# Attention with two mixtures of experts: products by low parts at the end of their group, and another spread of the next expert's weight split over a block

## The chip, the cores and the metric

The kernel runs on one core of a Trainium2 chip. The metric is the device time of one execution in microseconds, the median of several runs: 742.46 us before the change (three runs, 737.96 to 743.23). The engines' names: PE is TensorE (PEld its weight loads), DVE VectorE, ACT ScalarE, POOL GpSimd, SP SyncE, which issues most DMAs. PEq, ACTq and so on are the engines' sequencers, which run branches and semaphores.

## What is computed

Three stages in fp32. Attention over 2 batches of 8 heads, 1152 keys of 64 values, with the queries averaged in pairs; then two mixtures of experts over the 1152 tokens of 512 values that come out, each with 8 experts and a hidden width of 1024:

```python
attn = softmax(scale * q_pool @ k.transpose(0, 1, 3, 2))        # q_pool: queries averaged in pairs
x = rows(attn @ v)                                              # 1152 x 512
expert_idx = np.argmax(x @ w_gate, axis=1)                      # MoE 1, at most 288 tokens of an expert
h = np.maximum(np.einsum('ecd,edf->ecf', disp, w1), 0.0)
y = np.einsum('ecf,efd->ecd', h, w2)
out[i] = gate_w[i] * y[expert_idx[i], pos[i]]
do_compute = skip_score > 0                                     # MoE 2, with its own router
for e in range(E):
    h = np.maximum(xc[mask] @ w1[e], 0.0)
    y[mask] = gate_w[mask, None] * (h @ w2[e])
out[do_compute] = xc + y
```

## The kernel before

Attention takes the first 340 us or so, the experts of MoE 1 about 344 to 518, the last block of MoE 1 with the second router 518 to 565, and the experts of MoE 2 565 to 725. Then the last rows are written.

**Numbers in two parts.** The experts' products are made in fp32r, which keeps fewer bits, so each fp32 operand is held as a high part (its first twelve bits) and a low part (the rest). A product of two operands is the sum of three: high by high, high by low, low by high. For the tokens the parts are `xx[:, 0]` and `xx[:, 1]`, for the hidden layer `hh` and `hl`, for the weights the tiles `hi` and `lo` of each half (half 0 is w1, half 1 is w2).

**An expert's block.** `block_t` does up to 128 tokens of one expert. `first(hf)` lists the 12 products (4 chunks of the contraction, 3 parts) for one half of the hidden layer, and the relu behind them on ACT (L942, tile `hs`). `turn(hf)` transposes that half on PE (L948, `pg`), copies its high part on ACT (L950, `hh`) and takes the low part by subtraction on DVE (L951, `hl`). `second(py, hf)` lists the 12 products of that half by w2. PE's order in a block: first(0), half of first(1), turn(0), the rest of first(1), half of second(0), turn(1), a transpose of the next expert's tokens (`xprep`, L913 to L918, tiles `psx` and `xxn`), the rest of second(0), four products of second(1), a second such transpose (`xx`, for a second chunk of this expert), the other eight. The result is scaled on DVE (`yt`, L991 in MoE 1, L993 in MoE 2), the rows' places are worked out on DVE (`ix`, L883) and POOL issues the indirect DMA that writes the rows (L886).

**What fills a block.** Meanwhile the next expert's weights (four raw pieces of 1 MB, read by SP at L143) are split in 16 steps of 128x512. Step u copies the high part on ACT (L818, `hi`) and, one step behind, step u-1's low part is subtracted: on POOL for steps 0, 3, 6, 8, 11 and 14, on DVE for the other ten (L808, `lo`). Four steps use up one raw piece. The low part that ends a piece in half 0 issues the load that takes over its buffer; those of half 1 are kept back until after the branch. The steps are a list `fill`, and `flush(fill, n)` writes the next n of them into the program at that point. Each engine works its instructions off in the order in which they are written, and waits for other engines by semaphores; so the calls of `flush` set the order on ACT, DVE and POOL. The low parts that a `flush` puts out are one step behind the high parts.

**Between blocks.** Behind each expert's block stands a branch (L1172, in `experts`): if the expert has more than 128 tokens a second chunk follows, in `block_t` or, for up to 64 tokens, `block_h`. In this data that is so for experts 3 and 6 of MoE 1 and 6 of MoE 2. In the other eleven blocks that carry a split, the code of the second chunk is jumped over. `hs` has one buffer, and relu of the next block waits on ACT until DVE has passed L1172.

Of the kernel before, what the change touches and what calls it, by code (L numbers as in the profile page):

```python
# [8 lines left out]
F32 = mybir.dt.float32  # L9
F32R = mybir.dt.float32r  # L10
BF16 = mybir.dt.bfloat16
# [5 lines left out]
P = 128  # L17
# [4 lines left out]
def fused_kernel(  # L22
# [21 lines left out]
    KD = DM // P  # contraction chunks of the first product  # L44
    KF = F // P  # and of the second
    KC = S // P  # key chunks
    QP = 96  # rows of a chunk of queries, as loaded
    QC = SQ // QP
    CH = [P] * (SQ // P) + ([SQ % P] if SQ % P else [])  # token chunks of a batch
    NCH = len(CH)  # L50
    NT = B * NCH
    ROW = DM + 8  # a dispatched row: the token, its gate, its index
    REG = N  # rows of an expert's region
    NPRE = 3  # chunks of an expert that are read without an index
# [8 lines left out]
    # ---------------------------------------------------------------- constants  # L63
# [6 lines left out]
    rev = consts.tile([P, NT, E], F32, name="rev")  # E - e  # L70
# [10 lines left out]
    tri = consts.tile([P, P], BF16, name="tri")  # tri[k, m] = 1 where k < m  # L81
# [9 lines left out]
    def load_small(zeros):  # L91
        """Steps: the routers' weights, the capacity, zeros where tokens may be missing."""
# [22 lines left out]
        def capacity_value():  # L115
            # low + 2^32 * (high + (low < 0)), and not below 0
# [12 lines left out]
    # ---------------------------------------------------------------- weights  # L129
    RW = KD * F // 2  # words of a partition in one load: half of w1[e] or of w2[e]  # L130
# [15 lines left out]
    # ---------------------------------------------------------------- routing  # L146
# [5 lines left out]
    def masks(m):  # L152
        """1 in the rows of an expert's chunks that have no token."""
        nc.vector.tensor_tensor(
            out=mask[m],
            in0=cnt[m].unsqueeze(2).to_broadcast([P, E, NPRE]),
            in1=rowid.unsqueeze(1).to_broadcast([P, E, NPRE]),
            op=ALU.is_le,
        )

    def route(sp, ps_r, lg, nt, gate_out, prev, do=None, half_rows=()):
        """Three steps: the expert of each token, one-hot; its place among that expert's tokens; its gate.

        lg [P, nt, >= E] in SBUF; prev: one-hots of earlier tokens. The dictionary that is returned gets
        the one-hots (oh), the place (rank) and the first row of the expert's region (base).
        """
# [74 lines left out]
    def together(*lists):  # L241
        """The steps of several lists in turn."""
        n = max(len(x) for x in lists)
        for i in range(n):
            for x in lists:
                if i < len(x):
                    x[i]()

    def logits(m, rows, lg, ta, tb, xt, lt, groups, on_scalar=lambda j: j and j % 2, j0=0):
        """Steps to the logits of chunks of 128 tokens: for each group of chunks (each in a quadrant of the  # L250
        partitions) the transposes, the product and the way back."""
# [36 lines left out]
    def in_line(groups):  # L288
        """The steps of logits() in a row, a group's last ones behind the first transpose of the next."""
# [6 lines left out]
    def add_rows(ps, rows, places, first, last):  # L296
        """Adds to ps the transpose of the rows, each in its place: exact, by products with 0 and 1."""
# [10 lines left out]
    def places_of(place, oh):  # L308
        """One-hots of the tokens' places among an expert's first 128."""
# [3 lines left out]
    def count(ps_r, ohs, limit, m):  # L313
        """Tokens of each expert, on every partition, and in row 0 as integers."""
# [11 lines left out]
    def warm(ps, n):  # L326
        """Products that nobody reads: the array's clock would fall while it waits."""
# [24 lines left out]
    # ================================================================ attention  # L352
# [10 lines left out]
    def gate(b, ta, tb, groups):  # L363
        """Routing of a batch's tokens, and their rows to their experts' regions: steps to the logits, and the rest."""
# [31 lines left out]
    with ExitStack() as actx:  # L396
# [16 lines left out]
        PARTS = [(0, 2), (2, NCH)]  # chunks of the two halves of a pair's product with v  # L413
# [24 lines left out]
        def split0(n):  # L438
            """Sums of the pairs of queries, as far as the loads allow ahead."""
# [5 lines left out]
        def split1(n):  # L445
            """High and low parts of a head's keys and scaled queries, in twelve bits each: a list of steps."""
# [34 lines left out]
        def prep(n):  # L481
            """[high; low] of a head's keys, and [high; high], [low; low] of its queries, on the partitions."""
# [32 lines left out]
        def scores(n, c, it):  # L515
            """Scores of a chunk of queries with all keys; their maximum, exponentials and sums.

            The third piece of every chunk has a bank of its own, the others alternate.
            """
# [4 lines left out]
            def mm(j, part):  # L524
                # in the shared chunk the second head's queries have zeros in front of them
# [60 lines left out]
        def turn(n, c):  # L586
            """A chunk's weights with the keys on the partitions, in three groups."""
# [28 lines left out]
        def mix(i, part):  # L616
            """A pair of heads' product with v, turned to tokens on the partitions and divided by the sums."""
# [50 lines left out]
        # -------------------------------------------------------- the order of issue  # L668
# [25 lines left out]
        # The order of issue beside each of a pair's items, in the first pair and in the others: scores (s), the  # L694
        # maximum (m), the exponentials of the first pieces (f) and the last item's others (e), transposes of an
# [642 lines left out]
```

## Time and profile before

| what | us |
|---|---|
| runs: median (lowest to highest) | 742.46 (737.96 to 743.23) |
| span of the profiled execution | 734.7 |
| PE busy | 666.5 (91%) |
| DVE, ACT, POOL busy | 450.1, 433.3, 257.3 |
| lows on DVE (155) and POOL (101) | 157.2 and 142.0 |
| highs on ACT (256) | 141.5 |

The times are of one profiled execution, counted from the span's start. A row of an operation gives its line, the engine, output and inputs by the program's names, and shapes. Idle time is that of the engine just before the operation, with what ended it behind an arrow. PE's operations overlap their neighbours, so their starts are the better clock: two products in a row start about 0.23 us apart though each is listed with 0.4 us. Consecutive equal operations can stand in one row with their count.

### The profile page before, as it was taken

To read this page: it belongs to the slowest core of one execution; us is meant where nothing else is said; L and a number is where in the kernel's file an instruction comes from. 1 tells how busy PE (TensorE), PEld (TensorE's weight loads), DVE (VectorE), ACT (ScalarE), POOL (GpSimd) and SP (SyncE) were. 2 spreads that over 40 slices of the span, in tenths; PEclk is the share of its full clock that TensorE was granted. 3 is DMA by queue.
4 is the path that set the end of the run, shared out by engine and by line. 5 is a ranking of instruction groups with operands and counts; after the bars stand their busy time and mean duration, and the time that the engine had idled before them with its cause. 6 is when DMAs were issued, how large, how long until landed. Compare 5 with 4: busy or idle time off the path is not lost. (4 is left out here: it accounts for less than half of the span.)

```text
span 734.7 us, 11243 instructions
## 1 busy us (share of the span) xinstructions
PE 666.5 (91%) x3978; PEld 485.9 (66%) x3978; DVE 450.1 (61%) x729; ACT 433.3 (59%) x961; POOL 257.3 (35%) x240
## 2 busy tenths in 40 slices
PE   7999999999999999988888998899769888888994
PEld 6766667666767666646666766676648666666673
DVE  5755656565656664564888548842175788888211
ACT  5876767676757676651777347722350677776210
POOL 4322222222222520053566226510165566665010
PEclk8999999999999999999999999999988999999998
DMA  6042624050202122033889618850454798884100
GB/s 179 31 138 104 212 104 167 17 196 17 81 17 82 67 71 78 16 123 114 302 314 331 246 35 311 278 201 19 147 186 147 259 318 303 315 302 162 32 30 13
DMA packets 55599, 111.39 MB, mean 152 GB/s; under 512 B 5470, under 2 KB 14686, under 8 KB 55488
## 3 DMA queue, kind: packets, MB, share of 16 engines
q1 hardware_dynamic: 52128, 102.27, 40.8%
q0 software_dynamic: 3360, 7.72, 2.8%
q8 instruction: 59, 0.97, 0.5%
q14 instruction: 52, 0.43, 0.2%
HBM read 93.51 MB, written 19.71 MB: 154 GB/s over the span
## 5 line engine op out<-in xcount | busy, mean ns | idle before, releaser
L808 POOL TENSOR_TENSOR lo<-raw,hi 128x512 fp32r<-128x512 f32 x101 | 142.0, 1409 | 115.6 <-ACT hi L818 113.2
L808 DVE TENSOR_TENSOR lo<-raw,hi 128x512 fp32r<-128x512 f32 x155 | 157.2, 1065 | 4.3 <-ACT hi L818 4.3
L818 ACT CAST hi<-raw 128x512 fp32r<-128x512 f32 x256 | 141.5, 626 | 0.6 <-PE py L958 0.6
L527 PE MATMUL s_ps<-kop,qop 128*128 128x384 f32 x480 | 125.5, 369 | 1.7 <-ACT a L571 1.4
L555 DVE TENSOR_REDUCE m<-s_ps 128x1 f32<-128x1152 f32 x72 | 97.7, 1357 | 24.6 <-PE s_ps L527 22.4
L601 PE MATMUL pt<-ident,a 128*128 128x128 f32 x648 | 109.8, 283 | 3.2 <-ACT kop L476 1.1
L571 ACT ACTIVATE a<-s_ps,m 128x384 f32<-128x384 f32 (+1 forms) x144 | 106.8, 747 | 3.1 <-DVE m L555 2.9
L476 ACT COPY at<-pt 128x384 f32<-128x384 f32 x144 | 68.2, 481 | 64.0 <-PE pt L601 63.9
L601 PEld LDWEIGHTS pt<-ident,a 128*128 128x128 f32 x648 | 71.5, 140 | 45.9 <-ACT at L476 13.0
L627 PE MATMUL pv<-at,vr 128*64 128x320 f32 (+1 forms) x576 | 97.9, 428 | 0.0
L938 PE MATMUL ph<-hi,xxn 128*128 128x512 f32 x224 | 77.1, 405 | 13.1 <-PEq L1172 10.4
L476 DVE COPY at<-pt 128x384 f32<-128x384 f32 x72 | 39.8, 553 | 76.2 <-PE pt L601 74.1
L951 DVE TENSOR_TENSOR hl<-pg,hh 128x512 fp32r<-128x512 f32 x42 | 28.9, 687 | 89.0 <-ACT hh L950 89.0
L958 PE MATMUL py<-hi,hl 128*128 128x512 f32 x168 | 67.8, 404 | 12.5 <-DVE hl L951 12.5
L942 ACT ACTIVATE hs<-ph 128x512 f32<-128x512 f32 x42 | 25.1, 598 | 91.0 <-PE ph L938 52.3
L527 PEld LDWEIGHTS s_ps<-kop,qop 128*128 128x128 f32 x480 | 75.1, 187 | 5.3 <-ACT a L571 3.8
L958 PE MATMUL py<-hi,hh 128*128 128x512 f32 x168 | 68.7, 409 | 0.6
L886 POOL DMA_INDIRECT out_dram<-yt,ix x23 | 22.6, 981 | 133.0 <-DVE ix L883 81.7
L958 PE MATMUL py<-lo,hh 128*128 128x512 f32 x168 | 67.7, 403 | 0.0
L466 POOL TENSOR_TENSOR qhl<-qr,qhl 96x384 fp32r<-96x384 f32 x30 | 29.9, 1016 | 95.7 <-DVE qhl L464 95.7
L938 PEld LDWEIGHTS ph<-hi,xxn 128*128 128x128 f32 x224 | 42.1, 188 | 27.3 <-ACTq L1172 12.1
L454 POOL TENSOR_TENSOR khl<-kr_None,khl 128x576 fp32r<-128x576 f32 x14 | 19.8, 1414 | 87.2 <-DVE khl L453 87.2
(170 smaller groups left out, 948.2 us busy)
## 6 DMA issues: line engine op xcount, KB each, us to landing
raw<-in_moe_w_dram SPq DMA_DIRECT2D x64, 1024.0 KB, 6.0
x<-xs SPq DMA_DIRECT2D x36, 260.0 KB, 6.3
xs<-xtok SPq DMA_DIRECT2D x8, 780.0 KB, 7.4
qr<-in_q_dram SPq DMA_DIRECT2D x16, 288.0 KB, 3.2
vr<-in_v_dram SPq DMA_DIRECT2D x8, 576.0 KB, 6.0
kr_None<-in_k_dram SPq DMA_DIRECT2D x7, 576.0 KB, 5.0
out_dram<-xtok SPq DMA_DIRECT2D x3, 768.0 KB, 7.7
x<-out_dram SPq DMA_DIRECT2D x4, 512.0 KB, 6.3
```

What stands on the lines that cost most here:

```text
L466: sub.tensor_tensor(out=t[:, 1, :, r, :], in0=qs, in1=t[:, 0, :, r, :].bitcast(F32), op=ALU.subtract)
L476: (nc.vector.tensor_copy if on_vector else nc.scalar.copy)(dst, src)
L527: i = nc.tensor.matmul(s_ps[0:M, bank[j], 0 : 3 * P], qop[n + r][:, part, o : o + M], kop[n + r][:, j, :], start=(part == 0 and r == (c == ...
L555: i = nc.vector.tensor_reduce(out=nm, in_=s_ps[:, lo : lo + 3, 0 : 3 * P], axis=AX.XY, op=ALU.max, negate=True)
L571: i = nc.scalar.activation(a[:, a0 : a0 + nb, :], s_ps[:, b0 : b0 + nb, 0 : 3 * P], AF.Exp, bias=nm, accum_out=t[:, c, n % 2, k : k + 1],)
L601: nc.tensor.transpose(ps[:, x * P : (x + 1) * P], a[:, g, x * P : (x + 1) * P], ident)
L627: nc.tensor.matmul(hold["pv"][j * D : (j + 1) * D, 0:w], vrt[i][:, j, c * D : (c + 1) * D], at_t[2 * i + j, part][:, c, :], start=(c == 0) ...
L808: eng.tensor_tensor(out=lo, in0=raw, in1=hi.bitcast(F32), op=ALU.subtract)
L818: nc.scalar.copy(hi, raw)
L938: lambda d=d, i=i, a=a, b=b: nc.tensor.matmul(ps, xx[:, a, d, :], w1[b][:, d, s], start=(d + i == 0), stop=(d == KD - 1 and i == 2))
L951: nc.vector.tensor_tensor(out=hl[:, fs, :], in0=ps, in1=hh[:, fs, :].bitcast(F32), op=ALU.subtract)
L958: lambda f=f, i=i, a=a, b=b: nc.tensor.matmul(py, a[:, f, :], w2[b][:, f, :], start=(f + i == 0), stop=(f == KF - 1 and i == 2))
```

## The change

In `first` and `second` the loop over the three parts becomes the outer one: four products high by high, four by the other operand's low part, and then four by the tokens' (or the hidden layer's) low part, where they went in threes before. In the flow of a block, four steps of `fill` come ahead of the first product, then two (as before), one, one, two, three and the rest, where it was two, three, two, two, three and the rest. The rest of the difference takes comments out. In the numbering after the change, lines from 964 on are one higher (L1172 is L1173).

```diff
             def first(hf):
                 mms = []
-                for d in range(KD):
-                    for i, (a, b) in enumerate(((0, 0), (0, 1), (1, 0))):
+                for i, (a, b) in enumerate(((0, 0), (0, 1), (1, 0))):
+                    for d in range(KD):
                         mms.append(
                             lambda d=d, i=i, a=a, b=b: nc.tensor.matmul(
                                 ps, xx[:, a, d, :], w1[b][:, d, s], start=(d + i == 0), stop=(d == KD - 1 and i == 2)
...
             def second(py, hf):
                 mms = []
-                for f in range(hf * 4, hf * 4 + 4):
-                    for i, (a, b) in enumerate(((hh, 0), (hh, 1), (hl, 0))):
+                for i, (a, b) in enumerate(((hh, 0), (hh, 1), (hl, 0))):
+                    for f in range(hf * 4, hf * 4 + 4):
...
+            flush(fill, 4)
             mms, relu = first(0)
             flush(mms, 12)
             relu()
             flush(fill, 2)
             mms, relu = first(1)
             flush(mms, 6)
             turn(0)
-            flush(fill, 3)
+            flush(fill, 1)
             flush(mms, 12)
             relu()
-            flush(fill, 2)
+            flush(fill, 1)
             py = pa([P, DM], "py")
             mms = second(py, 0)
             flush(mms, 6)
             turn(1)
             flush(preps, 1)
             flush(fill, 2)
             flush(mms, 12)
             mms = second(py, 1)
             flush(fill, 3)
             flush(mms, 4)
             flush(preps, 1)
             flush(fill, len(fill))
             flush(mms, 12)
```

ACT in the first expert's block of MoE 1, from the block's first relu to its last high part, before (`hi_1_0` is the high part of expert 1's w1, `hi_1_1` of its w2):

```order
L942 ACTIVATE hs<-ph 128x512
L818 CAST hi_1_0_3845<-raw_1_0_0_3562 128x512 x2
L950 CAST hh<-pg 128x512
L818 CAST hi_1_0_3845<-raw_1_0_0_3562 128x512 x2
L818 CAST hi_1_0_3845<-raw_1_0_1_3590 128x512
L942 ACTIVATE hs<-ph 128x512
L818 CAST hi_1_0_3845<-raw_1_0_1_3590 128x512 x2
L950 CAST hh<-pg 128x512
L917 CAST xxn<-psx 128x512
L818 CAST hi_1_0_3845<-raw_1_0_1_3590 128x512
```

The same piece now:

```order
L818 CAST hi_1_0_3845<-raw_1_0_0_3562 128x512 x4
L942 ACTIVATE hs<-ph 128x512
L818 CAST hi_1_0_3845<-raw_1_0_1_3590 128x512 x2
L950 CAST hh<-pg 128x512
L818 CAST hi_1_0_3845<-raw_1_0_1_3590 128x512
L942 ACTIVATE hs<-ph 128x512
L818 CAST hi_1_0_3845<-raw_1_0_1_3590 128x512
L950 CAST hh<-pg 128x512
L917 CAST xxn<-psx 128x512
```

Four copies stand ahead of the first relu; between the first hh and the second relu there is one where there were three, between that relu and the second hh one where there were two.

DVE at the same place, a piece of the difference:

```order
-L951 TENSOR_TENSOR hl<-pg,hh 128x512
 L808 TENSOR_TENSOR lo_1_0_3846<-raw_1_0_0_3562,hi_1_0_3845 128x512 x2
-L808 TENSOR_TENSOR lo_1_0_3846<-raw_1_0_1_3590,hi_1_0_3845 128x512 x2
+L808 TENSOR_TENSOR lo_1_0_3846<-raw_1_0_1_3590,hi_1_0_3845 128x512
+L951 TENSOR_TENSOR hl<-pg,hh 128x512
+L808 TENSOR_TENSOR lo_1_0_3846<-raw_1_0_1_3590,hi_1_0_3845 128x512
 L951 TENSOR_TENSOR hl<-pg,hh 128x512
```

The first hl had four low parts behind it and now has three ahead of it; one stands between it and the second hl. POOL's order is as before.

PE at the end of the same block, from the second transpose of tokens (L913) to the branch (`hi_0_1` is the high part of expert 0's w2), before:

```order
L913 MATMUL psx<-ident,x_0_1_3843 128x128 x4
L958 MATMUL py<-lo_0_1_3538,hh 128x512
L958 MATMUL py<-hi_0_1_3537,hl 128x512
L958 MATMUL py<-hi_0_1_3537,hh 128x512
L958 MATMUL py<-lo_0_1_3538,hh 128x512
L958 MATMUL py<-hi_0_1_3537,hl 128x512
L958 MATMUL py<-hi_0_1_3537,hh 128x512
L958 MATMUL py<-lo_0_1_3538,hh 128x512
L958 MATMUL py<-hi_0_1_3537,hl 128x512
L1168 TENSOR_LOAD cnt_i_97
L1172 COMPARE_AND_BRANCH
```

And now, from the last part of the first group on:

```order
L958 MATMUL py<-hi_0_1_3537,hl 128x512 x4
L958 MATMUL py<-hi_0_1_3537,hh 128x512 x4
L913 MATMUL psx<-ident,x_0_1_3843 128x128 x4
L958 MATMUL py<-lo_0_1_3538,hh 128x512 x4
L958 MATMUL py<-hi_0_1_3537,hl 128x512 x4
L1169 TENSOR_LOAD cnt_i_97
L1173 COMPARE_AND_BRANCH
```

The products with hl were spread over each group, the first of them the third product; now they are its last four, and the branch follows them.

## Rows read from the trace of the kernel before

**Rows 1.** The page: span; busy time of TensorE, its share, its instructions.

```profile
span 734.7 us, 11243 instructions
...
PE 666.5 (91%) x3978; PEld 485.9 (66%) x3978; DVE 450.1 (61%) x729; ACT 433.3 (59%) x961; POOL 257.3 (35%) x240
```

**Rows 2.** Stretches: length, busy (count) of PE, PEld, DVE, ACT, POOL; clock, DMA, GB/s.

```profile
344.18:407.02 62.84, 54.97 (x256) 41.59 (x257) 52.37 (x63) 44.89 (x87) 38.95 (x29) 1.00 0.84 296
431.19:476.83 45.64, 40.73 (x193) 31.24 (x192) 36.38 (x45) 34.15 (x66) 26.97 (x20) 1.00 0.69 235
446.70:462.42 15.72, 13.66 (x65) 10.40 (x65) 13.29 (x18) 11.52 (x22) 9.54 (x8) 1.00 0.90 311
565.34:582.69 17.35, 13.93 (x65) 10.33 (x65) 12.67 (x18) 11.52 (x22) 10.85 (x9) 1.00 0.71 242
582.69:645.07 62.38, 54.64 (x256) 41.58 (x257) 51.11 (x64) 45.99 (x88) 37.18 (x28) 1.00 0.88 304
645.07:676.20 31.13, 28.02 (x131) 20.88 (x131) 26.38 (x34) 23.20 (x46) 19.00 (x15) 1.00 0.76 259
```

**Rows 3.** TensorE's waits, all of the span: us in total, times, longest.

```profile
PE py L958 <- DVE hl L951: 12.5, 13, 1.4
...
PE ph L938 <- PEq L1172: 10.4, 8, 2.5
...
PE psx L913 <- DMA x<-xs: 1.2, 1, 1.2
```

**Rows 4.** Block from 446.70, TensorE: start, us, operation, count, idle before and its releaser.

```profile
450.98 0.60 PE L948 MATMUL pg<-ident,hs 128*128 128x128 f32 x4
...
456.93 0.40 PE L958 MATMUL py<-lo,hh 128*128 128x512 f32 x1
...
458.25 0.51 PE L958 MATMUL py<-hi,hl 128*128 128x512 f32 x1 [0.92 <-DVE hl L951]
...
460.89 0.40 PE L958 MATMUL py<-hi,hl 128*128 128x512 f32 x1
...
462.42 0.47 PE L938 MATMUL ph<-hi,xxn 128*128 128x512 f32 x1 [1.13 <-PEq L1172]
```

**Rows 5.** Branch L1172 on TensorE's sequencer: ns min/median/max, first and last start.

```profile
L1172 PEldq COMPARE_BRANCH  x16: 70/3476/4270, 357.4 to 696.5; - x16
...
L1172 PEldq COMPARE_BRANCH  x1: 3833/3833/3833, 458.4 to 458.4; - x1
...
L1172 PEldq COMPARE_BRANCH  x1: 426/426/426, 388.8 to 388.8; - x1
...
L1172 PEldq COMPARE_BRANCH  x1: 4270/4270/4270, 578.3 to 578.3; - x1
```

**Rows 6.** The same block, VectorE, as in rows 4.

```profile
449.70 0.14 DVE L883 SCALAR_TENSOR_TENSOR ix<-mask,x 128x1 int32<-128x1 f32 x1
...
452.28 0.69 DVE L951 TENSOR_TENSOR hl<-pg,hh 128x512 fp32r<-128x512 f32 x1 [2.43 <-ACT hh L950]
...
452.89 4.70 DVE L808 TENSOR_TENSOR lo<-raw,hi 128x512 fp32r<-128x512 f32 x4
...
457.51 0.68 DVE L951 TENSOR_TENSOR hl<-pg,hh 128x512 fp32r<-128x512 f32 x1
```

**Rows 7.** The same block, GpSimd.

```profile
446.08 1.28 POOL L808 TENSOR_TENSOR lo<-raw,hi 128x512 fp32r<-128x512 f32 x1 [1.12 <-ACT hi L818]
...
455.41 1.63 POOL L808 TENSOR_TENSOR lo<-raw,hi 128x512 fp32r<-128x512 f32 x1 [0.69 <-ACT hi L818]
```

**Rows 8.** The same block, ScalarE.

```profile
450.02 0.60 ACT L942 ACTIVATE hs<-ph 128x512 f32<-128x512 f32 x1 [3.49 <-DVEq L1172]
450.51 1.13 ACT L818 CAST hi<-raw 128x512 fp32r<-128x512 f32 x2
```

**Rows 9.** Landing of raw weights (L143) from 440 to 480, then from 653 to 664.

```profile
DMA to landing us min/median/max: 5.0/5.0/6.5
...
DMA to landing us min/median/max: 7.2/8.0/8.8
```

## The prediction

> **What bounds the kernel now.** I read the page first, then a table of stretches, the waits of TensorE, the instructions of one expert's block on each engine, the branches, and the landings of the weights. The page gives 734.7 us of span with TensorE (PE) busy for 666.5 us, 91% [rows 1]: only its idle time can be won, and the change touches that of the expert blocks alone. The table of stretches [rows 2] cuts out the fourteen blocks that carry a split of the next weights: four of MoE 1 in 62.84 us, three in 45.64, the first of MoE 2 in 17.35, four in 62.38, two in 31.13. One alone (446.70 to 462.42) takes 15.72 us, of which PE is busy for 13.66. The list of PE's waits [rows 3] says where such blocks lose: 12.5 us in 13 waits of a product for hl on VectorE (DVE), and 10.4 us in 8 waits for the branch of L1172 at a block's end.
>
> In the block itself [rows 4] the first is the wait at 458.25: from 456.93 it is 1.32 us between two products that otherwise start 0.234 us apart (446.70 to 450.98 are 18 of them), so 1.09 us lost. The second is at 462.42: the last product started at 460.89, the next block's first could follow at 461.12, so 1.30 us are lost. Without both the block has 15.72 - 1.09 - 1.30 = 13.33 us.
>
> The branch needs a closer look, since it decides what a late hl costs. PE's sequencer runs ahead of its products and stops at waits. Its COMPARE_BRANCH at 458.4 took 3.83 us [rows 5], until 462.23; the first product of the next block is at 462.42. It stands about 0.2 us behind the release of the block's last wait, the one for its second hl, which ends at 458.19 [rows 6], while PE still had 2.7 us of products to do. At 388.8 it took 0.43 us; over all 16 of them 0.07 to 4.27 with a median of 3.48, the longest at 578.3. With 3.7 as what a long one takes, such a block can't end sooner than about 0.2 + 3.7 + 0.2 = 4.1 us after its **last wait** is released, wherever its products are.
>
> Why is hl late? DVE [rows 6] has the tail of the block before until ix ends at 449.84 (3.14 us into the block), is idle for 2.43 us until hl0 at 452.28, and then does four lows, 4.62 us, before hl1 at 457.51. PE's transposes for hl1 are the six products and a turn behind 452.6, so they were done some 2.5 us earlier. DVE starts the instruction behind hl0 0.61 us after it, so four lows alone would be 2.4 us; but two lows of GpSimd (POOL) fell into that time, one of them from 455.41 [rows 7], and each held a low of DVE. On ScalarE (ACT) [rows 8] it is alike: 3.49 us idle until relu0 at 450.02, which waits for DVE having passed L1172, and from then on a hi every 0.55 us. Both engines idle at a block's begin and are late in its middle.
>
> **The change part by part.** *No work is added or removed.* The same products, copies and lows run in another order; no operation is new and none changes its price.
>
> *Products.* In second(0) and second(1) the four hl products come last, so hl1 is wanted as product 9 of second(1) and not as product 3: six products and psx later, 6 x 0.234 = 1.4 us and up to 0.60 us for the transposes (as at 450.98 [rows 4]), as much as the 1.09 us that PE loses. hl0 gains the same six products, a turn and psx. In first() the products by the low part of the tokens come last too; for that I put nothing into the sum.
>
> *The split's steps.* Four stand at the block's begin, where ACT has 3.49 us idle; they take 4 x 0.55 = 2.2. Lows 1, 2 and 4 now stand ahead of hl0 on DVE, in its idle 2.43 us, and only one (5) between hl0 and hl1, where four were. I walk a block that follows another, t = 0 at its first product. ACT does hi0 to hi3 from 0 to 2.2. DVE's tail of the block before comes a little later than now, since the block before is shorter; I take ix at 3.8 where it was 3.14, and relu0 at 4.1 (now 3.3). PE is ready for the turn at 4.28 [rows 4] and has relu0's result at 4.7: 0.4 us late, a new loss. Then hi4, hi5, hh0 at 5.7, hl0 at 6.4, which PE needs at about 8.8. hi6, relu1 at 6.8; the second turn from 8.1, hh1 at 8.6, hl1 from 9.3 to 10.0, since DVE is through its one low by 8.9 at the latest (0.6 us, or 1.9 with a low of POOL ahead of it). Now hl1 ends at 458.19, t = 11.5.
>
> PE's products end at 13.33 + 0.4 = 13.7 with no wait for hl1 left. What ends the block is then the branch: from 10.2, behind the last wait, for 3.7 us, and the next first product is at about **14.1**. Where the branch is short (the blocks that end at 391.84 and 659.79, and those whose If is taken, which begin at 391.84, 462.42 and 659.79) I take 13.7.
>
> A floor lies just under this. A low of DVE and one of POOL don't run together, so ten of DVE at 0.60 and six of POOL at 1.28 (the undisturbed one [rows 7]) fill 10 x 0.60 + 6 x 1.28 = 13.7 us of a block. So 14.1 is possible, and much less is not.
>
> **Sum.** 344.18 to 407.02: first 15.3 (14.1 and the 1.2 us for its tokens' DMA [rows 3], which stay), then 14.1, 13.7, 13.7, so 56.8 from 62.84: 6.0. 431.19 to 476.83: 14.1 + 14.1 + 13.7 = 41.9 from 45.64: 3.7. First of MoE 2: with its branch of 4.27, 10.2 + 4.27 + 0.2 = 14.7 from 17.35: 2.6. 582.69 to 645.07: 4 x 14.1 = 56.4 from 62.38: 6.0. 645.07 to 676.20: the first at 13.7, the second less only the 1.09 us, 29.0 from 31.13: 2.1. Attention, router and last blocks: 0. Together 20.4: a span of 714.3 from 734.7. The median of the runs is 742.46, 7.8 us over this execution's span, and I keep that distance: **722 us**.
>
> **Bounds of what the trace doesn't show.** Below: eleven blocks of 14.1 to 15.3 at the floor of 13.7, 0.4 us each, 4.4 us: 718. Above: the raw weights. The next expert's first piece is asked for behind low 3 of a block, t about 8.7. hi0 may start until about 2.0 of the next block without holding relu0, so the piece has 14.1 + 2.0 - 8.7 = 7.4 us. It lands in 5.0 to 6.5 us in the stretch from 440, in 7.2 to 8.8 in the one from 653 [rows 9]. Each us over 7.4 lengthens a block by one: 8.0 gives 14.7, 8.8 gives 15.5 and nothing is won. The same bytes in 14.1 us instead of 15.72 are 311 x 15.72 / 14.1 = 347 GB/s for the block that has 311 [rows 2], above the 311 that I see held over a block, so I take the low row for the forecast (nearest in place to most blocks) and keep the high one for the range.
>
> **Rivals.** *A, the raw data come late*, as just worked out: 8.0 us everywhere costs 0.6 us in eleven blocks, 729; 8.5 costs 1.1, 734. For it: the 8.8 of rows 9. Against: the median of 5.0 in the stretch from 440. *B, the stall only moves.* relu0, behind a longer DVE tail and four hi, is late, PE's turn waits for it, and blocks stay at 15.3 to 15.7: 735 to 742. For it: relu0 waits for DVE already now. Against: DVE has 2.43 us idle behind that point, so its tail would have to be another 1.2 us longer than I walked. *C, the other side: the last wait now stands four products from the end.* Now the products behind hl1, 458.25 to 461.12, cover 2.9 us of the branch's 3.7; then four products cover 0.94. If hl1 ends no sooner than now, t = 11.5, the branch ends where it does now and nothing is won, and from there on every tenth of a us of hl1 is one of the block. At t = 12.1 eleven blocks are 0.6 longer: 6.6 us, 749. It decides at t = 11.5; my walk has 10.0. For it: hl0 stands behind three lows, each of which a low of POOL can hold for up to 1.28 us. Against: hl0 has 2.4 us of room, and hl1 has one low ahead of it. The Trainium skill ("Runtime: NRT & Kernel Launch", section Instruction fetch mechanics) speaks for C: a taken branch whose target is not in the window of fetched instructions forces a fetch before execution goes on. The trace agrees with 3.4 to 4.3 us where much code is jumped over, but has 0.43 us for the same line at 388.8, which the rule alone would not give; by the rule the two blocks with the short branch would be 14.1 as well and the time 723.
>
> **How the numbers follow.** The walk (717 to 726): 0.56. A (726 to 735): 0.21. B with the rest of A (735 to 743): 0.14. C (746 to 753): 0.09. The likeliest gives 722, its own range is 717 to 726. 716 to 738 leaves out C, the upper part of B and a little below. About 1% (7.4 us) is what a measurement of this kernel can tell from no change: faster is under 735.0, 0.77 by these cases; within 1% 0.14; slower 0.09.
>
> **What would show it.** After the change: the waits of py for hl gone or under 2 us; a block's hl1 at t = 9 to 10; ACT's idle time at a block's begin gone, hi0 to hi3 ahead of relu0; waits PEq L1172 still there, 0.3 to 0.8 us each, in blocks of about 14.1; landings of raw under 7.4 us. It is wrong if hl1 still holds PE four products before the end (C), if the turn waits for relu0 by over 1 us (B), if ACT's hi0 waits for the DMA (A), or if the branch is shorter or longer than 3.4 to 4.3 us, which moves all blocks where the If is not taken.

## The result

The changed kernel takes 729.42 us (median of four runs, 728.32 to 732.65) and the kernel before, beside it, 742.85 (737.96 to 743.39): a ratio of 0.985, with a 95% interval of 0.981 to 0.989. That is 13.4 us. The forecast was 722 and 20.4 us less, range 716 to 738.

The profiled execution has a span of 727.8 us, 6.9 less than [rows 1]. It is the run of 729.55 us, so a run is 1.75 us longer than its span. A later trace of the kernel before has 735.3 us of span for a run of 737.05, the same distance.

The page of the kernel after, the span and busy time as in [rows 1]:

```profile
span 727.8 us, 11259 instructions
...
PE 665.6 (91%) x3978; PEld 491.2 (67%) x3978; DVE 456.3 (63%) x729; ACT 436.8 (60%) x961; POOL 262.2 (36%) x240
```

Stretches of the kernel after, columns as in [rows 2], cut at the same places of the program:

```profile
344.35:406.77 62.42, 54.89 (x256) 43.34 (x257) 56.51 (x63) 46.41 (x88) 38.81 (x29) 0.97 0.84 296
430.04:473.87 43.83, 41.39 (x194) 32.74 (x192) 38.57 (x44) 34.86 (x66) 28.01 (x20) 0.96 0.72 244
443.87:459.28 15.41, 13.41 (x64) 10.46 (x65) 14.77 (x19) 11.69 (x23) 11.55 (x8) 1.00 0.97 344
564.45:580.07 15.62, 13.65 (x65) 10.48 (x65) 12.05 (x17) 11.59 (x22) 10.69 (x9) 1.00 0.68 238
580.07:640.27 60.20, 54.57 (x257) 43.25 (x257) 52.66 (x65) 46.85 (x88) 39.42 (x29) 0.97 0.93 322
640.27:669.19 28.92, 27.00 (x131) 21.33 (x131) 25.95 (x33) 23.71 (x46) 20.39 (x15) 1.00 0.80 281
```

Against [rows 2]: 62.84 became 62.42, 45.64 became 43.83, the single block 15.72 became 15.41, 17.35 became 15.62, 62.38 became 60.20, 31.13 became 28.92. So each stretch is shorter, but the first four blocks, with 6.0 us forecast, give 0.4. The DMA share of the single block went from 0.90 to 0.97.

PE's waits after, as in [rows 3]:

```profile
PE ph L938 <- PEq L1173: 12.2, 8, 2.2
...
PE psx L913 <- DMA x<-xs: 1.8, 1, 1.8
...
PE pg L948 <- ACT hs L942: 1.6, 3, 0.7
...
PE py L958 <- DVE hl L951: 1.5, 2, 1.3
```

The waits for hl are down from 12.5 us to 1.5, as forecast. Those for the branch, forecast at 0.3 to 0.8 us each, did not fall; they rose from 10.4 us to 12.2, the longest 2.2.

The same steady block as in [rows 4], which now begins at 443.87, on PE, then on DVE ([rows 6]), then on ACT ([rows 8]):

```profile
448.41 0.66 PE L948 MATMUL pg<-ident,hs 128*128 128x128 f32 x4
...
453.05 1.09 PE L958 MATMUL py<-hi,hl 128*128 128x512 f32 x4
...
456.29 1.09 PE L958 MATMUL py<-hi,hl 128*128 128x512 f32 x4
...
459.28 1.13 PE L938 MATMUL ph<-hi,xxn 128*128 128x512 f32 x2 [1.91 <-PEq L1173]
```

```profile
447.44 0.14 DVE L883 SCALAR_TENSOR_TENSOR ix<-mask,x 128x1 int32<-128x1 f32 x1
...
447.89 3.01 DVE L808 TENSOR_TENSOR lo<-raw,hi 128x512 fp32r<-128x512 f32 x3 [0.31 <-DVEq L1173]
...
450.83 0.68 DVE L951 TENSOR_TENSOR hl<-pg,hh 128x512 fp32r<-128x512 f32 x1
...
452.95 0.69 DVE L951 TENSOR_TENSOR hl<-pg,hh 128x512 fp32r<-128x512 f32 x1 [0.32 <-ACT hh L950]
```

```profile
444.11 2.18 ACT L818 CAST hi<-raw 128x512 fp32r<-128x512 f32 x4 [0.19 <-ACTq L1173]
447.75 0.60 ACT L942 ACTIVATE hs<-ph 128x512 f32<-128x512 f32 x1 [1.46 <-DVEq L1173]
```

hl1 ends at 452.95 + 0.69 = 453.64, t = 9.77; it was 11.5. PE takes up its last four products at 456.29 without waiting, and they are over at 457.4. Then it stands until 459.28. The branch on PE's sequencer, as in [rows 5], all of them and then the one of this block:

```profile
L1173 PEldq COMPARE_BRANCH  x16: 70/3362/5742, 356.9 to 689.3; - x16
...
L1173 PEldq COMPARE_BRANCH  x1: 5413/5413/5413, 453.7 to 453.7; - x1
```

The branch began 0.06 us behind hl1, at 453.7, and took 5.41 us where its counterpart of before took 3.83. It ends at 459.11, and this is what ends the block.

### The profile page after: what moved, and what is told of

Same layout as the page of the kernel before. It is cut to its first block, busy times and chain, and to the rows that moved or that the text cites. A ratio compares the mean times of both kernels' runs of the same rounds, so it can differ in the third digit from the quotient of the medians.

```text
span 727.8 us, 11259 instructions
## 1 busy us (share of the span) xinstructions
PE 665.6 (91%) x3978; PEld 491.2 (67%) x3978; DVE 456.3 (63%) x729; ACT 436.8 (60%) x961; POOL 262.2 (36%) x240
## 5 line engine op out<-in xcount | busy, mean ns | idle before, releaser
L808 POOL TENSOR_TENSOR lo<-raw,hi 128x512 fp32r<-128x512 f32 x101 | 145.7, 1456 | 104.0 <-ACT hi L818 100.8
L808 DVE TENSOR_TENSOR lo<-raw,hi 128x512 fp32r<-128x512 f32 x155 | 160.9, 1080 | 13.9 <-ACT hi L818 10.5
L818 ACT CAST hi<-raw 128x512 fp32r<-128x512 f32 x256 | 143.0, 623 | 12.0 <-PEq L1173 4.7
L938 PE MATMUL ph<-hi,xxn 128*128 128x512 f32 x224 | 62.7, 412 | 14.9 <-PEq L1173 12.2
L958 PE MATMUL py<-lo,hh 128*128 128x512 f32 x168 | 52.5, 414 | 0.0
L958 PE MATMUL py<-hi,hh 128*128 128x512 f32 x168 | 46.8, 400 | 1.4 <-ACT hh L950 0.8
L958 PE MATMUL py<-hi,hl 128*128 128x512 f32 x168 | 46.2, 396 | 1.5 <-DVE hl L951 1.5
```

What stands on the lines that cost most here:

```text
L808: eng.tensor_tensor(out=lo, in0=raw, in1=hi.bitcast(F32), op=ALU.subtract)
L818: nc.scalar.copy(hi, raw)
L938: lambda d=d, i=i, a=a, b=b: nc.tensor.matmul(ps, xx[:, a, d, :], w1[b][:, d, s], start=(d + i == 0), stop=(d == KD - 1 and i == 2))
L958: lambda f=f, i=i, a=a, b=b: nc.tensor.matmul(py, a[:, f, :], w2[b][:, f, :], start=(f + i == 0), stop=(f == KF - 1 and i == 2))
```

## The experiments

Besides the times I compare one stretch of the traces in all kernels: from PE's first product of the first expert's block to the first product of MoE 2's expert 7 (344.18 to 686.86 before, 344.35 to 679.75 after). Attention ahead of it varies by up to 6 us between executions of kernels that are the same there (343.1 to 348.9 at its end), and that variation is left out in this way.

| kernel | median, us | ratio to before (95%) | stretch, us |
|---|---|---|---|
| before | 742.85 | | 342.68 |
| before, second trace | 738.26 | 1.000 (0.998 to 1.002) | 342.72 |
| changed | 729.42 | 0.985 (0.981 to 0.989) | 335.40 |
| changed, second trace | 725.94 | 0.987 (0.979 to 0.994) | 332.03 |
| only the products' order | 743.36 | 1.007 (1.004 to 1.010) | 347.45 |
| only the split's steps | 739.20 | 0.999 (0.997 to 1.002) | 345.89 |
| changed, without the branch | 725.01 | 0.980 (0.976 to 0.985) | 331.02 |
| changed, lows 3 and 4 swapped | 730.45 | 0.988 (0.983 to 0.992) | 335.06 |
| changed, steps 4, 1, 2, 1 | 728.51 | 0.986 (0.982 to 0.990) | 336.16 |
| changed, both | 730.85 | 0.990 (0.986 to 0.993) | 332.42 |
| changed, first() in threes | 726.87 | 0.986 (0.981 to 0.990) | 331.84 |
| changed, first() in threes and 4, 1, 2, 1 | 729.71 | 0.989 (0.984 to 0.994) | 333.72 |

Each ratio is to runs of the kernel before beside it; their medians were 738.25, 738.46 and 738.68 in the three sessions behind the first. Differences of 2 or 3 us between the changed kernel and its variants are no more than it shows against itself.

### Each half of the change alone

The products' order alone (the fill as before):

```diff
-            flush(fill, 4)
             mms, relu = first(0)
...
-            flush(fill, 1)
+            flush(fill, 3)
             flush(mms, 12)
             relu()
-            flush(fill, 1)
+            flush(fill, 2)
```

> Only the order of the products is changed; the split's steps stand as before. Theory 1 (the spread of the steps makes hl early, the order alone can't): hl1 ends at t = 11.5 to 12 of a block as before, PE no longer stands for over 0.5 us at a product for hl, but the long branch begins 0.2 us behind hl1 and its wait grows to 2 us or more; blocks 15.5 to 15.8 us, the time within 4 us of before (739 to 747). Rival (the 1.4 to 2.0 us of room for hl1 are the whole gain): 13 waits of 1.09 us go, the branches' waits stay at 10 us in all, about 729.

The steps alone (the products in threes as before):

```diff
-                for i, (a, b) in enumerate(((0, 0), (0, 1), (1, 0))):
-                    for d in range(KD):
+                for d in range(KD):
+                    for i, (a, b) in enumerate(((0, 0), (0, 1), (1, 0))):
...
-                for i, (a, b) in enumerate(((hh, 0), (hh, 1), (hl, 0))):
-                    for f in range(hf * 4, hf * 4 + 4):
+                for f in range(hf * 4, hf * 4 + 4):
+                    for i, (a, b) in enumerate(((hh, 0), (hh, 1), (hl, 0))):
```

> Only the split's steps are moved; the products go in threes as before. Theory 1: hl1 ends at t = 9.5 to 10.2 as in the changed kernel, before PE wants it as product 3 of second(1) (t about 10.5), hl0 at t = 7 to 7.5 is late by 0.5 to 1 us in some blocks since it is wanted at 6.6; the branch's waits as in the changed kernel (10 to 13 us); 729 to 735. Rival (both parts are needed): hl0's wait takes all of it back, 738 to 745.

PE's waits, us in total, times, longest, with the order alone:

```profile
PE ph L938 <- PEq L1172: 17.6, 8, 2.6
...
PE pg L948 <- ACT hs L942: 3.5, 3, 1.5
```

And with the steps alone:

```profile
PE ph L938 <- PEq L1173: 12.1, 9, 2.8
...
PE py L958 <- DVE hl L951: 7.8, 10, 2.4
...
PE ph L938 <- issue: 6.8, 4, 3.9
```

The order alone makes the kernel slower, 743.36 to 738.25. This is rival C of the prediction in pure form: no wait for hl is left in the list's upper rows, but the branch begins behind the same hl1 as before (at 458.2 in a block that begins at 446.63, t = 11.5) and nothing covers it any more, so its waits grow from 10.4 to 17.6 us. Theory 1 had that; the time lies in its 739 to 747, though it is 5.1 us over the kernel before beside it where within 4 had been said, and the stretch is 4.8 us longer than before. Two of its blocks, from 597.68 and 614.70, last 17.0 and 17.1 us: behind 2.46 and 2.10 us of waiting for the branch, the clock granted to PE was at 0.50 there for some 3 us. It fell so at the begin of five blocks that carry a split, and of none in the kernel before, so the clock may have a part in the loss.

The steps alone bring nothing, 739.20 to 738.25, and here theory 1 failed and its rival held: hl0, behind three lows, comes after the third product of second(0) wants it, and ten waits for hl take 7.8 us; hl1 is early, but the branch's waits are 12.1 us, and four waits of PE for which the profile shows no releaser ("issue") add 6.8, of it 6.4 in the middle of three blocks. So each half alone gives nothing or a loss, and both together 7 to 11 us of the stretch and about 13 of the medians: the order of the products gives hl0 its room, and the steps bring hl1, and with it the branch, forward.

### What makes the branch long

Nine branches were long in the first trace of the kernel before, 3.36 to 4.27 us. In the changed kernel five of the nine took 4.90 to 5.74. Two theories: it shares the DMA with the raw weights, or it is longer because it begins sooner. The changed kernel without the raw loads from expert 2 on:

```diff
         seq_at[0] += 1
+        if seq_at[0] > 8:
+            raw_t[m, e, half, r] = raw_t[0, 1, half, r]
+            return
```

> The changed kernel without the loads of raw weights from expert 2 of the first mixture on: the split reads expert 1's raw pieces again, so all other work stays. Theory 1 (the fetch behind the long branch shares the DMA with the raw pieces; 3.3 to 3.4 us where the queues fall idle within the branch, 4.9 to 5.7 where they stay full): every long branch takes 3.2 to 3.5 us, blocks of 14.0 to 14.3, the time 715 to 722. Theory 2 (the branch takes longer because it begins earlier, whatever the DMA does): some of them stay at 4.9 or more, every second one above 4.5, 726 to 732.

The time, 685.16 us, is no measure of the loads alone: other tokens are routed to the experts of MoE 2, and fewer chunks are left at its end (3,818 products on the page and not 3,978). The blocks up to 630 are the same work. The branches (all from 436.5 on: ns min/median/max), PE's waits for them, and the stretches as in [rows 2], the first four blocks and then three, one and four:

```profile
L1176 PEldq COMPARE_BRANCH  x12: 70/3424/4002, 436.5 to 669.3; - x12
```

```profile
PE ph L941 <- PEq L1176: 3.0, 5, 1.0
```

```profile
343.10:402.87 59.77, 53.71 (x257) 42.01 (x257) 55.88 (x64) 46.30 (x88) 38.31 (x29) 1.00 0.26 86
426.15:467.53 41.38, 39.93 (x193) 31.49 (x192) 38.45 (x44) 34.74 (x66) 28.86 (x20) 1.00 0.12 36
560.27:574.28 14.01, 13.22 (x65) 10.58 (x65) 11.78 (x16) 11.57 (x22) 8.16 (x7) 1.00 0.32 97
574.28:630.52 56.24, 53.66 (x257) 41.88 (x257) 51.59 (x64) 46.02 (x88) 39.95 (x28) 1.00 0.14 41
```

The long branches of these blocks take 2.94 to 3.72 us (a later one 4.00), though in steady blocks they begin as early, t = 9.5 to 10.5, as the five of the changed kernel that took 4.90 or more, t = 9.5 to 10.4. The waits for the branch are 3.0 us instead of 12.2. The last three stretches are 41.38, 14.01 and 56.24 us; the forecast had 41.9, 14.7 and 56.4. Theory 2 falls: beginning early does not make it long. So without raw loads the forecast's walk comes out in these eight blocks, though not in the first four (in the first of which the last loads still land): they take 59.77 us where 56.8 was forecast, and PE waits 1.30 and 1.29 us for an hl0 behind three lows in two of them. The four stretches together are 171.4 us, 182.1 in the changed kernel and 169.8 in the forecast: the loads account for most of what is missing. They can do so by more than the branch, since ACT's waits for raw pieces go with them too.

With every second raw load left out:

```diff
+        if seq_at[0] > 8 and r == 1:
+            raw_t[m, e, half, r] = raw_t[0, 1, half, r]
+            return
```

> The changed kernel with every second load of a raw piece left out from expert 2 of the first mixture on (the split reads expert 1's pieces in their place): half the weights' traffic, all other work as it was. In the second mixture other tokens are routed, so only blocks and branches are compared. Theory 1 (traffic in the queues lengthens the fetch): DMA share of a block near 0.5, branches of 3.3 to 4.3 us in nearly all blocks, blocks of 13.7 to 14.5. Theory 2 (the branch is longer because it begins sooner): branches of 4.9 us and more in every second block, blocks of 15.

Neither theory's numbers: half the traffic, and still four branches of 4.78 to 5.42 us. (The time, 689.49 us, is no measure here either.) One of them, and the load of raw (L146 in this kernel's numbering) that was issued ahead of it and the one behind it (first and last start, us):

```profile
L1176 PEldq COMPARE_BRANCH  x1: 5113/5113/5113, 451.3 to 451.3; - x1
```

```profile
L146 SPq DMA_DIRECT2D raw<-in_moe_w_dram x2: 378/378/379, 449.7 to 455.8; - x2
```

The one piece that was under way was issued at 449.7, 1.6 us ahead of the branch at 451.3, and the branch took 5.11. So it is less the mean load of the queues that counts than a piece that was issued shortly ahead. With this in mind the traces of the two unchanged kernels (two each) sort themselves. In the steady blocks of the kernel before the last raw piece was issued 3.0 to 3.1 us ahead of the branch: 3.58 to 3.90 us. In the kernel after, where it was issued 1.5 to 2.4 us ahead: 4.76 to 5.41 us, eight branches; 0.8 and 1.2 us ahead: 5.98 and 5.74; 3.5 us or more ahead: 3.32 to 3.91, six branches, and 4.32 and 4.46 at the first block of MoE 2. Left out of this are nine short branches, 0.32 to 1.61 us, two of them with a piece issued 2.0 and 2.3 us ahead. Which block has a short one differs between executions of the same kernel: the branch at 641.2 took 3.72 us in the first trace of the kernel before, its counterpart at 641.6 in the second 0.43; why, no run shows. For the steady block shown above and its counterpart of before, the issue of the raw piece on SP's queue, before and after:

```profile
L143 SPq DMA_DIRECT2D raw<-in_moe_w_dram x1: 378/378/378, 455.3 to 455.3; - x1
```

```profile
L143 SPq DMA_DIRECT2D raw<-in_moe_w_dram x1: 378/378/378, 452.1 to 452.1; - x1
```

Low 3 releases that load: at 455.3, t = 8.6, before, and at 452.1, t = 8.2, after. The branch went from t = 11.7 to t = 9.8. It moved by 1.9 us and the load by 0.4, and so it fell into the load.

Three branches don't fit: at the second block of three kernels (368.8, 369.2 and 370.0) a piece had been issued 0.8 to 1.2 us ahead, and they took 3.08 to 3.40 us, where others took 5.5 to 6.1 at the same place. Perhaps the fetch was queued ahead of the piece there; no run shows it, and that stays open.

### The branch by itself

The changed kernel with the If left out for the eleven experts that carry a split and have no second chunk:

```diff
-                with tc.If(n_e > P):
...
+                if (m, e) not in [(0, 0), (0, 1), (0, 2), (0, 4), (0, 5)] + [(1, k) for k in range(6)]:
+                    with tc.If(n_e > P):
...
```

> The changed kernel with the branch for a second chunk left out for the eleven experts that carry a split and have none (and with it the relu's and the scatter's wait for VectorE having passed it), so the price of the branch by itself. Theory 1 (after the change the branch ends the blocks): PE's waits for it (12.2 us) go, blocks are 13.7 to 14.0, bounded by the lows that exclude each other, 714 to 720. Rival (the lows of VectorE and GpSimd bound the blocks already at 15): a wait for hl or hs takes its place and the time stays at 726 to 731.

725.01 us, 4.4 and 0.9 less than the two medians of the changed kernel (in the stretch 4.4 and 1.0 less than its two traces): neither the 714 to 720 of theory 1 nor quite the nothing of its rival. PE's waits for hl, ACT's waits for the raw pieces, and two steady blocks:

```profile
PE py L958 <- DVE hl L951: 11.1, 9, 1.7
```

```profile
ACT hi L818 <- DMA raw<-in_moe_w_dram: 9.7, 11, 2.3
```

```profile
603.76:618.35 14.59, 13.23 (x65) 10.54 (x64) 14.59 (x17) 11.81 (x23) 9.00 (x7) 1.00 0.95 331
618.35:632.94 14.59, 13.22 (x66) 10.55 (x65) 14.59 (x17) 11.75 (x23) 9.00 (x7) 1.00 0.92 332
```

Without the branch these two blocks take 14.59 us each (the others 13.4 to 15.5). The next two limits are just behind it: the raw pieces, for which ACT waits 11 times (rival A, 9.7 us in all), and hl0, 11.1 us in 9 waits, since its three lows start late and GpSimd holds them. In both rows DVE is busy for all of the 14.59 us, and PE waits 1.36 and 1.37 us for hl0. So the branch alone is worth 1 to 4 us of the stretch and not the 12.2 that PE waits for it; what the branch and hl0 are worth together no run shows, since none takes out both. The late hl0 is to be seen in the changed kernel too, in the block from 391.32: DVE's lows and hl0, POOL's lows, and PE's wait, as in [rows 4]:

```profile
395.90 5.94 DVE L808 TENSOR_TENSOR lo<-raw,hi 128x512 fp32r<-128x512 f32 x3 [0.31 <-DVEq L1173]
401.77 0.68 DVE L951 TENSOR_TENSOR hl<-pg,hh 128x512 fp32r<-128x512 f32 x1
```

```profile
396.89 3.79 POOL L808 TENSOR_TENSOR lo<-raw,hi 128x512 fp32r<-128x512 f32 x3
```

```profile
402.50 1.20 PE L958 MATMUL py<-hi,hl 128*128 128x512 f32 x4 [1.28 <-DVE hl L951]
```

Three lows of DVE took 5.94 us, since three of POOL's ran one behind the other in that time. hl0 began at t = 10.45 and ended at 11.1, where the walk had it ready at 6.4, and this block lasted 15.45 us where 13.7 were forecast.

### Edits that should have moved the load or the lows

Low 3 on DVE (so that the piece is issued sooner), low 4 on POOL; fewer steps ahead of hl0; both; the first half of the reordering undone; and that with the fewer steps:

```diff
-        ON_POOL = (0, 3, 6, 8, 11, 14)
+        ON_POOL = (0, 4, 6, 8, 11, 14)
```

> The changed kernel with low 3 on VectorE and low 4 on GpSimd, so that the load of the next expert's first raw piece (which low 3 releases) starts about 2 us earlier in a block, in one steady block at t = 6 to 7 and not at 8.2. Theory 1 (the fetch behind the branch is slow while raw pieces fill the DMA queues): the piece has landed soon after the branch begins, a gap opens, long branches take 3.3 to 4.5 us instead of 4.9 to 5.7, blocks 14.4 to 14.8, time 720 to 726. Theory 3 (not the branch but the lows of the two engines set the block of 15): no gain, 727 to 733, with hl0 late by over 1 us in most blocks, since VectorE has the same number of lows ahead of it.

```diff
             relu()
-            flush(fill, 2)
+            flush(fill, 1)
             mms, relu = first(1)
             flush(mms, 6)
             turn(0)
-            flush(fill, 1)
+            flush(fill, 2)
```

> The changed kernel with one step behind the first relu and two behind the first turn (4, 1, 2, 1 instead of 4, 2, 1, 1): two lows ahead of hl0 on VectorE and two between hl0 and hl1. Theory 1 (the long branch, begun behind hl1, ends the blocks): hl0's waits go, but hl1 comes up to 0.6 us later where a low of GpSimd holds VectorE, the branch with it; within 4 us of the changed kernel's 729. Theory 3 (hl0 behind three lows is what holds the blocks): 721 to 726.

> Both edits together: low 3 on VectorE, low 4 on GpSimd, steps 4, 1, 2, 1. VectorE's order is that of the swap alone, ScalarE reaches hh0 one copy (0.55 us) sooner. Theory 1: as with the swap alone, 719 to 726. Theory 3: 0.5 us a block less than with the swap alone.

```diff
-                for i, (a, b) in enumerate(((0, 0), (0, 1), (1, 0))):
-                    for d in range(KD):
+                for d in range(KD):
+                    for i, (a, b) in enumerate(((0, 0), (0, 1), (1, 0))):
```

> The changed kernel with the products of first() in threes again and only those of second() by parts: the piece of the change for which nothing stood in the sum. Expected: within 3 us of the changed kernel, 727 to 733, with the 0.6 us waits for xx back at the second chunks. Rival (the order in first matters too, since the low parts of the tokens and of w1 are ready late at a block's begin): waits for xx or lo at a block's begin in many blocks, 734 or more.

> The changed kernel with the products of first() in threes and the steps as 4, 1, 2, 1: the two edits that took nothing away, together. If each wait that they remove counts: 722 to 726, with the waits for hl0 and xx both under 2 us in all. If the blocks are held at 14.5 to 15.5 by the fetch behind the branch and by the DMA queues: 726 to 730, no different from either edit alone.

All five lie between 726.87 and 730.85, at or just above the changed kernel's own two medians, 725.94 and 729.42, and within its runs, 725.45 to 734.54. The swap moved the load to t = 5.6 to 7.6 in steady blocks (6.5 to 8.8 in the changed kernel), less than had been meant, and so brought the piece to 2.7 to 3.9 us ahead of the branch in steady blocks, and the branches took 4.26 to 5.80 us there, once 6.87 and once 3.47. At 3.0 us ahead the kernel before had 3.6 to 3.9, so the distance to the piece ahead does not give the length alone, and theory 1 got the time wrong (720 to 726 expected, 730.45 measured). One difference is to be seen over all the traces with loads. With the last piece issued 2.5 to 3.2 us ahead, the 22 long branches for which the piece before it had been issued 9 us or more ahead took 3.58 to 4.12 us; of the 26 for which it had been issued 6.7 to 8.7 us ahead, as behind the swap, 23 took 4.04 to 6.87 and three 3.62 to 3.78. So a second piece under way seems to count as well; no run changes this alone. The steps 4, 1, 2, 1 cut the longest wait for hl0 from 1.28 us to 0.7, but there was little to win, 1.5 us in two waits before the edit and 1.4 in two behind it, and the time stayed where it was: this speaks against theory 3, that hl0 holds the blocks, only as long as the branch is there. PE waited 5.1 us with no releaser shown, 4.7 of it in the middle of two blocks. Both edits together gave 730.85, the time of neither theory. Undoing the order in first() costs nothing, as expected: the time's gain is all from second() and the steps. With the steps 4, 1, 2, 1 on top of that the time was 729.71, so the removed waits did not count there either. None of them beats the changed kernel by more than its traces differ among themselves.

### The two kernels once more

> The kernel before, unchanged, for a second trace of it. If the first trace was a typical one: its eight long branches take 3.3 to 4.3 us again, nearly all blocks lose 1.09 us to hl1, the stretch from the first expert block to the second mixture's expert 7 is 342 to 344 us (342.68 in the first trace), and where the runs differ by some us the difference lies ahead of the first expert block.

> The changed kernel, unchanged, for a second trace of it. If contention decides on a branch's length: the branches that find the DMA queues full take 4.5 us or more again, though not always at the same blocks, and the stretch from the first expert block to the second mixture's expert 7 is within 3 us of 335.4. If the first trace was an odd one: branches of 3.3 to 4 us throughout and a stretch near the 322 that the forecast's sum gives.

The kernel before repeats itself: 342.72 us in the stretch (342.68 in the first trace), hl1's waits at 12.2 us, long branches of 3.39 to 3.90. The changed kernel has 332.03 us, 3.4 from the first trace's 335.40 where within 3 had been expected, and five steady-block branches between 4.76 and 5.98 us again, at 369.4, 453.2, 586.3, 600.8 and 615.7; the first trace was not an odd one.

## Why the forecast held and where its sum was off

The time lies in the range and the way was right, but the gain is two thirds of the forecast (13.4 us of 20.4), and 729.42 is outside the 717 to 726 of the walk (the second median, 725.94, just inside); it lies where rival A stood (726 to 735), by another mechanism. That the range held is so in part luck. By the prediction's own signs it was wrong in one: the long branch was to stay within 3.4 to 4.3 us. In the stretch the forecast's 20.4 became 7.3 us in the first pair of traces and 10.7 in the second.

- **hl1 early, hl's waits gone: right.** hl1 was walked to end at t = 10.0 and ended at 9.77; relu0 at 4.1 and came at 3.88; the waits are 1.5 us, "under 2".
- **hl0 at 6.4 with 2.4 us of room: too good.** It was ready at 7.6 (450.83 + 0.68) in the steady block shown and at 11.1 in the one from 391.32, where three lows of POOL held the lows ahead of it and PE waited 1.28 us. The walk had let POOL hold one low between hl0 and hl1, but none of the three ahead of hl0. Rival C named just this.
- **The branch from 10.2 for 3.7 us: the step that failed.** The place was right (9.8) and the length was not. I took 3.7 us from a table in which each branch of a steady block stands 3 us behind the load of a raw piece, and moved the branch by 1.9 us without looking at what it would then run beside. Behind a piece issued 1.5 to 2.4 us ahead it took 4.76 to 5.41 us. That is 1.1 to 1.7 us over the 3.7, and in the first trace the five steady blocks that end in a branch of 4.90 us or more last 14.59 to 15.66 us where 14.1 was forecast; these five branches are 8.0 us over the forecast's price together, of the 13.1 by which the stretch fell short of it. Without the loads three of the four stretches come out within 0.7 us of the forecast, and the first four blocks 3.0 us over it. The Trainium skill ("Runtime: NRT & Kernel Launch", section Instruction fetch mechanics) says that a taken branch out of the fetched window needs a DMA fetch. I used it for where the price falls. That the fetch is a DMA is in the same sentence. That it is slower beside the DMA of the weights is not; this is inferred from the branch's length, 2.94 to 4.00 us in the run without loads and 4.76 to 5.98 in the changed kernel behind a piece issued shortly ahead.
- **The first four blocks: 0.4 us for 6.0.** The trace of after has 16.65, 15.44, 14.88 and 15.45 us there, forecast 15.3, 14.1, 13.7 and 13.7. The first waits 1.84 us for its tokens' DMA (1.2 before): that wait stays at the same time, while PE comes earlier. The second has the 5.74 us branch, the third its slow clock (below), the fourth the late hl0.
- **Rival A, as a wait of ACT for raw data: seen once in the changed kernel (2.0 us), 11 times without the branch.** In the changed kernel the branch may hide it: ACT's first copy of a block waits for PE having passed the branch, 4.7 us in five waits.
- **Router and last block: 0 forecast, 1.4 us lost.** 518.84 to 565.34 was 46.50 us and is 47.94 (516.51 to 564.45); 46.81 and 47.52 in the second traces. PE waits 0.81 us for an hh there that it didn't wait for, and 1.19 us instead of 0.29 for a one-hot of the router; but this second wait was 2.86 in the second trace of the kernel before and 0.96 in that of the changed one, so it need not be the change's.
- **The distance of 7.8 us between span and median.** It is none: a run is 1.75 us longer than its own span, so the first trace of before is of an execution of about 736.5 us, 1.5 less than the quickest run of then. The medians differ by 13.4 and 12.7 us and the spans of the traces by 6.9 and 11.5; forecast were 20.4 for both. The median of 742.46, from which the forecast was counted, was itself high: the later ones of the kernel before are 738.25 to 738.68, and counted from there the forecast would have been 718.

## What to carry to other kernels

When a wait is taken away, ask not only what the freed engine does next but what that next thing will run beside: here a branch moved 1.9 us forward and into the DMA of a 1 MB weight piece and became 1.1 to 1.7 us longer, as much as most of the 1.6 us that the forecast gave such a block. A duration that is read from a trace holds for the neighbours that it had there. And two halves of a change can each be worth nothing or less and still bring 13 us together, so a half that is tried alone is no test of the whole.

## What the runs showed of the chip that I had not expected

A branch on PE over the code of a second chunk took 2.94 to 4.00 us with no weight loads, 3.6 to 3.9 in the kernel before behind a 1 MB load issued 3 us ahead, and 4.8 to 6.0 in the changed kernel behind one issued 0.8 to 2.4 us ahead. Over all the traces with loads, 21 of 24 long branches with a load issued less than 2.4 us ahead took 4.76 to 6.14 us, and the other three 3.08 to 3.40.

PE's clock fell at three of the changed kernel's block begins, behind idle times of 2.24, 1.91 and 1.85 us there. The clock granted around the first of them (the column ahead of the last two), as in [rows 2]:

```profile
375.00:376.40 1.40, 0.00 (x0) 0.00 (x0) 1.40 (x2) 0.00 (x0) 1.11 (x1) 1.00 1.04 395
376.44:377.40 0.96, 0.96 (x4) 0.82 (x5) 0.96 (x3) 0.52 (x1) 0.00 (x0) 1.00 0.96 378
377.40:378.40 1.00, 1.00 (x4) 0.75 (x4) 1.00 (x2) 1.00 (x3) 0.00 (x0) 0.51 0.93 301
378.40:379.40 1.00, 1.00 (x4) 0.81 (x3) 0.69 (x3) 0.66 (x2) 0.53 (x1) 0.50 1.05 410
379.40:380.40 1.00, 1.00 (x3) 0.75 (x3) 1.00 (x2) 0.00 (x0) 0.97 (x2) 0.50 1.08 369
380.40:381.40 1.00, 1.00 (x5) 0.77 (x4) 1.00 (x1) 0.29 (x1) 1.00 (x2) 0.78 1.06 262
381.40:382.40 1.00, 1.00 (x7) 0.78 (x6) 1.00 (x1) 1.00 (x3) 1.00 (x1) 1.00 1.02 291
```

For about 3 us from 377.4 on, the granted clock is 0.50 of the higher level, 1.2 GHz and not 2.4, and products start 0.43 us apart (377.45 to 379.16 are four). Before the change no block that carries a split had this, though one began behind 2.52 us of idle time, and in the second trace of the changed kernel none had it, though one began behind 2.48; so the idle time alone does not decide it. It costs less than it looks: in the block from 595.11 the later products put the branch 4.5 us behind the raw load, it took 3.40 us, and the block was 14.91 us long.
